# A fused attention and two-MLP kernel: each attention lane packs all its units before it unpacks them

## The chip, the core and the metric

The kernel runs on one core of one Trainium2 chip. The metric is the device time of one execution in microseconds (us). The engines are PE (TensorE matmul), PEld (its weight load), DVE (VectorE), ACT (ScalarE), POOL (GpSimd) and SP (SyncE, which issues every DMA here). Each works through its own program in order, and semaphores hold an instruction until what it reads is there.

## The reference

Shapes: q, k, v are 4 x 8 x 576 x 64 and p is 4 x 8 x 32 x 64 (batch, head, token, depth).

```python
def sm_attn(qq, kk, vv):
    s = scale * qq @ kk.T;  s = s - max(s);  a = exp(s)
    return (a / (sum(a) + 1e-9)) @ vv
p_packed = sm_attn(p, k, v)                  # "pack":   32 rows attend to 576
x = sm_attn(q, p_packed, p_packed)           # "unpack": 576 rows attend to 32
x = x.transpose(0, 2, 1, 3).reshape(2304, 512)
h = x @ w_in;  x = (h * sigmoid(1.702 * h)) @ w_out       # first MLP, 512 -> 2048 -> 512
pr = domain_probs / (domain_probs.sum(-1) + 1e-9)         # second MLP: four experts
out = sum(pr[:, e] * (relu(x @ w1[e]) @ w2[e]) for e in range(4))
```

w_in and w_out come as 64-bit floats, which the kernel turns into pairs of 32-bit numbers ("conversions").

## The kernel before

The attention is cut into eight units: a unit is one batch and four of its heads. Unit u has two steps. `pack(u)` (written p0 to p7) turns k with PE (tile kT), takes scores against pT (ps_s), the maximum on DVE (st), the exponential on ACT, turns the result back (ps_e), multiplies it with v (ps_v), divides on DVE (pp) and turns that once more (ps_pt). `unpack(u)` (u0 to u7) does the like for q (qT, then t on DVE), takes the exponential on ACT, multiplies on POOL and leaves the tile a, cast on ACT (L446) and finished on DVE (L448).

A conversion works on one 512 KB piece of w_in or w_out: six DVE operations (all write the tile cvt), one on POOL, a cast on ACT and a subtraction on POOL. Eight pieces serve the first quarter of the hidden width, four more follow in the same lane (`MORE`).

The first MLP runs in four rounds, one for a quarter of the hidden width, and eight half-batches j in a round. `packed_w` (ps_w) multiplies the packed rows of four units with w_in, ACT and DVE copy it out (pw, L482 and L486); `l1_first` (ps_h) multiplies that with the tiles a of the two units of a batch, ACT applies the gelu twice (L516, L517), DVE subtracts (h, L520); `l2_first` (ps_acc) multiplies with w_out, and ACT copies into y. A half-batch is four groups of 6 ps_h and 12 ps_acc matmuls.

The order in which these stand in the engines' programs is made when the program is written. The class `Order` keeps several parts side by side: two attention lanes (`LANES`), a lane of conversions and the lane of the first MLP. Each part says which engine it wants next and for how long by its own table; `Order.run` takes the one that can start first, and a lower rank on ties. The instructions are then written in that order for all engines ("the head"); after it a scheduler or a fixed loop takes over. All loads are issued by SP in one order (`FIRST`, then as lanes ask for them). Tiles of the pool `big` (29 slots) are handed out in the same order, and a load waits in SP's queue until its slot is free.

In the kernel before, a lane packs two units and unpacks them, then does the same with its other two. The probabilities are loaded by `norm_probs`, which is written after the head, but its load stands second in SP's program.

Of the kernel before, what the change touches and what calls it, by code (L numbers as in the profile page):

```python
# [19 lines left out]

LANES = ("p0 p2 u0 u2 p4 p6 u4 u6", "p1 p3 u1 u3 p5 p7 u5 u7")
FIRST = "k0 k1 F F F F k2 k3 q0 q1 F F F F"
HOP = 0.25
UNITS_DONE = 6
MORE = 4


class Order:

    def __init__(self, banks):
        self.free = banks
        self.at = {}
        self.parts = []
        self.on = False

    def add(self, part, rank, at=0.0):

        if not self.on:  # L40
            return self.drain(part)
        self.parts.append([rank, at, next(part, None), part])

# [8 lines left out]
    def run(self, while_):  # L52
        self.on = True
        while while_():
            best = None
            for p in self.parts:
                rank, at, ask, part = p
                if callable(ask):
                    t = ask()
                    if t is None:  # L60
                        continue
                    p[1] = max(at, t)
                    p[2] = self.send(p, p[1])
                    best = p
                    start = None
                    break
# [6 lines left out]
            if start is None:  # L73
                continue
            assert best is not None, [p[2] for p in self.parts]
            (start, _), p = best
            engine, us, banks = p[2]
            self.free -= banks
            self.at[engine] = start + us
            p[1] = start + us + HOP  # L80
            p[2] = self.send(p, p[1])
        self.on = False
# [15 lines left out]
def packed_attention_moe_kernel(  # L98
# [13 lines left out]
    nc = tc.nc  # L112
# [33 lines left out]
    def slot(shape, dt, name):  # L146
        return big.tile(shape, dt, tag="b", name=name)
# [49 lines left out]
    def convert():  # L197
# [12 lines left out]
        f32 = man.bitcast(F32)  # L210
        yield "DVE", 0.83, 0

# [6 lines left out]
        )  # L219
        yield "DVE", 1.2, 0  # L220
        nc.vector.tensor_scalar(
# [25 lines left out]
    def load_kv(u):  # L247

        b, g = units[u]
        h0 = G * g  # L250
        sl = [slot([SP, 3 * R * D], F32, f"kv{u}{i}") for i in range(3)]
        m = 2 * R * D
        raws["k", u] = []
# [11 lines left out]
        raws["v", u] = [sl[0][:, m:], sl[1][:, m:], sl[2][:, :R * D], sl[2][:, R * D:m]]  # L265

# [12 lines left out]
    def transposed_scores(pair, dst, scores):  # L279

        for s in range(2):
            for j in range(2):
                yield "PE", 0.4, 1
                ps = psum("ps_t")
                for r in range(3):
                    nc.tensor.transpose(ps[:, r * SP:(r + 1) * SP], pair[j][3 * s + r], ident[:SP, :SP])
                t = yield "ACT", 0.4, 0
                nc.scalar.copy(out=dst[:, j, s * HS:(s + 1) * HS], in_=ps[:, :HS])
                order.free += 1
        for s in range(2):  # L290
            yield "PE", 0.6, 1
            yield from scores(s)
# [39 lines left out]
    def pack(u):  # L332
        b, g = units[u]
        kr, vr = raws.pop(("k", u)), raws.pop(("v", u))
        st = small.tile([128, 8], F32, tag="st", bufs=4, name=f"st{u}")
        kT = slot([128, 2, S], F32, f"kT{u}")
# [13 lines left out]
        for s in range(2):  # L350
            yield "ACT", 0.7, 0
            nc.scalar.activation(
# [10 lines left out]
        for s in range(2):  # L363
            yield "PE", 0.45, 1
            ps = psum("ps_e")
# [6 lines left out]
            order.free += 1  # L372
        yield "PE", 1.0, 1
        ps = psum("ps_v")
# [40 lines left out]
    def unpack(u):  # L415
# [17 lines left out]
        nc.vector.tensor_sub(out=t, in0=t, in1=s2[:, 0, :].unsqueeze(2).to_broadcast([128, NB, NP]))  # L433
        yield "ACT", 0.7, 0
        nc.scalar.activation(out=t, in_=t, func=AF.Exp, scale=scale)
# [23 lines left out]
    def packed_w(a, bp):  # L459

        for g in range(UG):
# [11 lines left out]
            for b in (2 * bp, 2 * bp + 1):  # L473
                PW[a, b, g] = slot([128, 2, 512], F32R, f"pw{g}")
            order.add(packed_w_out(a, bp, g, pss), 1, clock())

# [16 lines left out]
    def l1_first(a, j, c):  # L493
# [16 lines left out]
        h = hid[a, j, c // 2][:, 2 * (c % 2):2 * (c % 2) + 2, :]  # L510
        order.add(l1_out(h, ps), 1, clock())

    def l1_out(h, ps):
# [5 lines left out]
        yield "DVE", 0.47, 0  # L519
        nc.vector.tensor_sub(out=h[:, 1, :], in0=g32, in1=h[:, 0, :].bitcast(F32))  # L520

    def l2_first(a, j, t):
# [21 lines left out]
        order.add(l2_out(a, j, t, ps), 1, clock())  # L544

# [245 lines left out]
    def reads(fn, args):  # L791
# [6 lines left out]
        return [("out", args[0], c) for c in range(CPP)]  # L798

# [68 lines left out]
    with tc.manual_schedule(engines=engines):  # L868
# [15 lines left out]
    norm_probs()  # L884
    t_parts = {i: t_sums(i) for i in range(NPAIR)}
# [71 lines left out]
```

## Time and profile before

| | us |
|---|---|
| median of 3 runs (lowest to highest) | 1238.83 (1236.79 to 1240.83) |
| profiled execution: its time | 1239.21 |
| profiled execution: span of the trace | 1237.4 |
| PE busy (matmul), of the span | 1174.5 (95%) |
| DVE busy | 913.6 (74%) |
| ACT busy | 522.9 (42%) |
| POOL busy | 486.5 (39%) |

An engine's busy time is the union of its instructions. Matmuls are pipelined, so a busy PE can still be slow: the granted clock (1.00 is 2.4 GHz, 0.50 is 1.2 GHz, a number between is a mean over both) has to be read beside it. Windows are given in us from the start of the span.

### The profile page before, as it was taken

Reading aid. Unit: us, or ns where it says so; the run is one execution under the profiler, and the core shown is the slowest. Engines: PE = TensorE matmul, PEld = TensorE weight load, DVE = VectorE, ACT = ScalarE, POOL = GpSimd, SP = SyncE. Lnnn points to the kernel's source line nnn. Section 1 sums busy time; section 2 is a strip of 40 time slices with the busy share of each in tenths; the row PEclk is TensorE's granted clock in tenths of the full one; section 3 lists DMA queues with packets and bytes.
Section 4 is the critical chain, followed back from the end, with each engine's and each line's share of the span. In section 5 each row is a group of like instructions: output and inputs, shape, how many; then the busy total and the mean of one; then the engine's idle time right before and its main releaser. Section 6 shows DMA issues by size and latency. Waiting matters only on the chain.

```text
span 1237.4 us, 18457 instructions
## 1 busy us (share of the span) xinstructions
PE 1174.5 (95%) x6912; PEld 1059.5 (86%) x6912; DVE 913.6 (74%) x1646; ACT 522.9 (42%) x1152; POOL 486.5 (39%) x415
## 2 busy tenths in 40 slices
PE   6769878999999989999999999999999999999998
PEld 4457667999999989999999989999999789999997
DVE  4873478787786675777777977777778867777775
ACT  3557654444434444333333344333333443333331
POOL 1320023221121244444444765444447644444441
PEclk9879789999999999999999999999999999999999
DMA  8623212120210002222222132222221232222211
GB/s 233 181 77 78 73 52 85 52 69 18 80 40 18 1 17 69 68 68 69 69 69 68 51 110 95 69 68 68 69 69 35 67 121 69 69 69 69 68 52 51
DMA packets 90393, 87.47 MB, mean 71 GB/s; under 512 B 43968, under 2 KB 71616, under 8 KB 90304
## 3 DMA queue, kind: packets, MB, share of 16 engines
q1 hardware_dynamic: 90304, 86.30, 23.3%
q8 instruction: 54, 0.88, 0.3%
q14 instruction: 35, 0.29, 0.1%
HBM read 81.56 MB, written 4.72 MB: 70 GB/s over the span
## 4 chain that ended last, share of the span: by engine, by line
PE 76%; DVE 4%; ACT 2%; issue 1%; POOL 0%; DVEq 0%
PE ps_o L726 30%; PE ps_p L674 27%; PE ps_acc L528 12%; PE ps_h L500 6%; DVE b L609 1%; PE ps_w L468 1%; ACT h L682 1%; DVE o L737 1%; ACT b L608 0%; DVE s L643 0%; DVE h L520 0%; ACT w L153 0%; DVE h L683 0%; POOL w L154 0%; DVE u L700 0%
## 5 line engine op out<-in xcount | busy, mean ns | idle before, releaser
L726 PE MATMUL ps_o<-w,h 128*128 128x512 f32 x1728 | 444.5, 393 | 0.0
L674 PE MATMUL ps_p<-b,w 128*128 128x384 f32 x2016 | 402.9, 338 | 4.9 <-POOL w L154 2.6
L674 PEld LDWEIGHTS ps_p<-b,w 128*128 128x128 f32 x2016 | 360.1, 188 | 32.1 <-POOL w L154 4.6
L726 PEld LDWEIGHTS ps_o<-w,h 128*128 128x128 f32 x1728 | 321.9, 188 | 50.2
L154 POOL TENSOR_TENSOR w<-raw,w 128x512 fp32r<-128x512 f32 x192 | 230.1, 1198 | 227.8 <-ACT w L153 222.9
L737 DVE SCALAR_TENSOR_TENSOR o<-ps_o,pr,o 128x512 f32<-128x512 f32 x270 | 201.5, 746 | 48.0 <-PE ps_o L726 48.0
L528 PE MATMUL ps_acc<-h,wout 128*128 128x288 f32 x1536 | 231.6, 298 | 5.0 <-DVE h L520 5.0
L528 PEld LDWEIGHTS ps_acc<-h,wout 128*128 128x128 f32 x1536 | 213.7, 190 | 9.3 <-DVE h L520 6.4
L154 POOL TENSOR_TENSOR w<-s,w 128x512 fp32r<-128x512 f32 x96 | 125.2, 1304 | 164.3 <-ACT w L153 164.3
L500 PE MATMUL ps_h<-a,pw 128*128 128x288 f32 x768 | 129.0, 303 | 17.4 <-ACT a L446 12.6
L500 PEld LDWEIGHTS ps_h<-a,pw 128*128 128x128 f32 x768 | 112.5, 193 | 21.2 <-ACT a L446 13.4
L520 DVE TENSOR_TENSOR h<-g,h 128x288 fp32r<-128x288 f32 x128 | 73.0, 572 | 61.9 <-ACT g L517 61.5
L153 ACT CAST w<-s 128x512 fp32r<-128x512 f32 x96 | 58.9, 614 | 126.0 <-DVE s L646 126.0
L153 ACT CAST w<-raw 128x512 fp32r<-128x512 f32 x192 | 106.6, 555 | 1.7 <-DMA raw<-in_moe_w_dram 1.6
L516 ACT ACTIVATE h<-ps_h 128x288 fp32r<-128x288 f32 x128 | 53.1, 415 | 105.2 <-PE ps_h L500 104.7
L217 POOL TENSOR_SCALAR cvt<-cvt 128x512 uint32<-128x512 uint32 x32 | 23.9, 747 | 128.7 <-DVE cvt L214 110.2
L682 ACT ACTIVATE h<-c 128x384 fp32r<-128x384 f32 x48 | 25.3, 527 | 106.9 <-DVE c L708 106.9
L682 ACT ACTIVATE h<-u 128x384 fp32r<-128x384 f32 x48 | 25.2, 525 | 71.6 <-DVE u L714 71.6
L553 DVE TENSOR_TENSOR y<-ps_acc,y 128x288 f32<-128x288 f32 (+2 forms) x120 | 44.8, 389 | 12.9 <-PE ps_acc L528 12.7
L682 ACT ACTIVATE h<-uv 128x384 fp32r<-128x384 f32 x48 | 25.3, 526 | 67.2 <-DVE uv L714 67.2
L643 DVE TENSOR_TENSOR s<-raw 128x256 f32<-128x256 f32 x48 | 45.1, 941 | 10.4 <-DMA raw<-in_moe_w_dram 10.4
L517 ACT ACTIVATE g<-ps_h 128x288 f32<-128x288 f32 x128 | 52.6, 411 | 0.1
(100 smaller groups left out, 1162.9 us busy)
## 6 DMA issues: line engine op xcount, KB each, us to landing
raw<-in_moe_w_dram SPq DMA_DIRECT2D x96, 512.0 KB, 4.0
raw<-in_moe_w_in_dram SPq DMA_DIRECT2D x16, 512.0 KB, 3.9
raw<-in_moe_w_out_dram SPq DMA_DIRECT2D x16, 512.0 KB, 3.7
kv<-in_k_dram SPq DMA_DIRECT2D x32, 144.0 KB, 3.2
q<-in_q_dram SPq DMA_DIRECT2D x32, 144.0 KB, 2.8
out_dram<-o SPq DMA_DIRECT2D x18, 256.0 KB, 2.0
kv<-in_v_dram SPq DMA_DIRECT2D x16, 144.0 KB, 3.0
kv<-in_v_dram SPq DMA_DIRECT2D x8, 288.0 KB, 3.4
```

Of the source, the lines that this page charges most:

```text
L153: nc.scalar.copy(out=hi, in_=src)
L154: eng.tensor_sub(out=lo, in0=src, in1=hi.bitcast(F32))
L500: nc.tensor.matmul(out=ps[:, :HS], lhsT=PW[a, b, g][:, wp, c * 128:(c + 1) * 128], rhs=A[b * UG + g][:, xp, s * HS:(s + 1) * HS], start=(m ...
L516: nc.scalar.activation(out=h[:, 0, :], in_=ps[:, :HS], func=AF.Gelu_apprx_sigmoid)
L517: nc.scalar.activation(out=g32, in_=ps[:, :HS], func=AF.Gelu_apprx_sigmoid)
L520: nc.vector.tensor_sub(out=h[:, 1, :], in0=g32, in1=h[:, 0, :].bitcast(F32))
L528: nc.tensor.matmul(out=ps[:, :HS], lhsT=W["out", a, c][:, wp, t * 128:(t + 1) * 128], rhs=hid[a, j, c // 2][:, 2 * (c % 2) + hq, :], start ...
L643: nc.vector.tensor_add(out=s1, in0=Am["A21"], in1=Am["A22"])
L674: nc.tensor.matmul(out=ps, lhsT=Wop[n, a, wp, kk], rhs=Bop[i, b, xp, kk], start=(m == 0), stop=(m == 5),)
L682: nc.scalar.activation(out=h[:, 0, :], in_=src, func=AF.Relu)
L726: nc.tensor.matmul(out=ps, lhsT=h[:, c, hq, o:o + 128], rhs=W2[n, c][:, wp, :], start=(c == 0 and m == 0), stop=(c == 1 and m == 2),)
L737: nc.vector.scalar_tensor_tensor(out=acc, in0=ps, scalar=pr[:, tok, e:e + 1], in1=acc, op0=ALU.mult, op1=ALU.add,)
```

## The change

Each lane now packs its four units and then unpacks them. `Order` looks for the earliest start plus a handicap per part instead of breaking ties by rank, adds 1.28 us of its own reckoning where an ACT step would need another function table than the last one ("exp" or "gelu"), and a part whose condition is met is no longer served at once. Some of the planner's table times are changed. The k and v of units 0, 1 and 2 are loaded into the three buffers of the pool `yp`, which later hold y, so nine of the 29 slots of `big` stay free at the start. The pool `small` has 4 buffers instead of 2. The load of the probabilities moves behind the loads of `FIRST`, and `norm_probs` runs after the head. No arithmetic is changed. The program has 8 table loads on ACT where it had 18.

```diff
-LANES = ("p0 p2 u0 u2 p4 p6 u4 u6", "p1 p3 u1 u3 p5 p7 u5 u7")
+LANES = ("p0 p2 p4 p6 u0 u2 u4 u6", "p1 p3 p5 p7 u1 u3 u5 u7")
+EARLY = (0, 1, 2)
+TABLE = 1.28
...
-                engine, us, banks = ask
+                engine, us, banks, table = (p[2] + (None,))[:4]
                 if banks > self.free:
                     continue
-                start = max(at, self.at.get(engine, 0.0))
-                if best is None or (start, rank) < best[0]:
-                    best, start_ = ((start, rank), p), start
+                start = max(p[1], self.at.get(engine, 0.0))
+                late = TABLE if table not in (None, self.table) else 0.0
+                if best is None or start + late + p[0] < best[0]:
+                    best = start + late + p[0], start + late + us, p
...
-    small = ctx.enter_context(tc.tile_pool(name="small", bufs=2))
+    small = ctx.enter_context(tc.tile_pool(name="small", bufs=4))
...
-        yield "DVE", 1.2, 0
+        yield "DVE", 1.5, 0
...
+        if u in EARLY:
+            t = yp.tile([128, KD, 2 * TB], F32, tag="y", name=f"kv{u}").rearrange("p k t -> p (k t)")
+            sl = [t[:SP, x * 3 * n:(x + 1) * 3 * n] for x in range(2)] + [t[:SP, 6 * n:8 * n]]
+        else:
+            sl = [slot([SP, 3 * n], F32, f"kv{u}{i}") for i in range(3)]
...
-            yield "ACT", 0.7, 0
+            yield "ACT", 0.7, 0, "exp"
...
-        yield "ACT", 0.82, 0
+        yield "ACT", 0.82, 0, "gelu"
...
     def norm_probs():
-        nc.sync.dma_start(out=pr, in_=probs.rearrange("(t p) e -> p t e", p=128))
...
         load(FIRST)
+        nc.sync.dma_start(out=pr, in_=probs.rearrange("(t p) e -> p t e", p=128))
         order.on = True
         lanes = [lane(x) for x in LANES] + [conversions(2 * CPP, MORE)]
-        for i, x in enumerate(lanes):
-            order.add(x, 2 + i)
-        order.add(moe_lane(), 9)
+        for x in lanes[:-1]:
+            order.add(x, 0.0)
+        order.add(lanes[-1], 0.6)
+        order.add(moe_lane(), 0.3)
```

Three places show what the new order does (the digit behind kT, q, kv, pp, t or a is the unit, what follows the underscore is a serial number).

PE behind the last matmul of unit 3's pack (ps_pt of pp3), before the change:

```order
L400 MATMUL ps_pt_565<-ident_76,pp3_557 128x128
L286 MATMUL ps_t_573<-ident_76,q0_160 128x96 x3
L297 MATMUL ps_s_588<-qT0_508,pT_78 64x288 x2
L286 MATMUL ps_t_592<-ident_76,q1_163 128x96 x3
L468 MATMUL ps_w_597<-win_181,ppw0_302 128x512 x3
L468 MATMUL ps_w_601<-win_252,ppw0_302 128x512 x3
L297 MATMUL ps_s_611<-qT0_508,pT_78 64x288 x2
```

The same place after it:

```order
L407 MATMUL ps_pt_567<-ident_76,pp3_560 128x128
L293 MATMUL ps_t_576<-ident_76,kv40_395 128x96 x3
L293 MATMUL ps_t_585<-ident_76,kv41_396 128x96 x3
L293 MATMUL ps_t_592<-ident_76,kv50_428 128x96 x3
L475 MATMUL ps_w_610<-win_176,ppw0_308 128x512 x3
L475 MATMUL ps_w_614<-win_253,ppw0_308 128x512 x3
L304 MATMUL ps_s_620<-kT4_524,pT_78 64x288 x2
```

The unpacks of units 0 and 1 stood here; now the packs of units 4 and 5 do, and those of units 6 and 7 behind them. Counting matmuls further on, the last score of an unpack stands behind 114 ps_h, 168 ps_acc and 24 ps_w matmuls before, and behind 84, 120 and 12 after; from the second round of the MLP on, PE's order is the same in both.

ACT at the exponentials (L352) of the pack of unit 4, before:

```order
L352 ACT_TABLE_LOAD
L352 ACTIVATE kT4_882,st4_881<-ps_s_976,st4_881 128x288
L352 ACTIVATE kT4_882,st4_881<-ps_s_992,st4_881 128x288
L288 COPY kT5_1009<-ps_t_1011 128x288
L516 ACT_TABLE_LOAD
```

And after:

```order
L489 CAST pw1_642<-ps_w_637 64x512
L359 ACTIVATE kT4_524,st4_523<-ps_s_620,st4_523 128x288
L295 COPY kT5_583<-ps_t_665 128x288
L359 ACTIVATE kT4_524,st4_523<-ps_s_646,st4_523 128x288
L378 COPY kv40_395<-ps_e_694 96x384
```

No gelu stands before or between them any more, so the two table loads are gone. The unpacks keep three of these pairs of loads.

DVE behind the last division of unit 5's pack (pp5), before the change:

```order
L387 SCALAR_TENSOR_TENSOR pp5_1286<-ps_v_1256,st5_1008,mask2_77 128x128
L343 TENSOR_REDUCE st6_1143<-ps_s_1283 128x1
L347 TENSOR_SCALAR st6_1143<-st6_1143 128x1
L358 TENSOR_SCALAR st6_1143<-st6_1143 128x1
L361 RECIPROCAL st6_1143<-st6_1143 128x1
L520 TENSOR_TENSOR h_1248<-g32_1331,h_1248 128x288
```

And after:

```order
L394 SCALAR_TENSOR_TENSOR pp5_800<-ps_v_767,st5_582,mask2_77 128x128
L214 TENSOR_SCALAR cvt_795<-raw_169 128x512
L215 TENSOR_SCALAR cvt_795<-cvt_795 128x512
L222 TENSOR_SCALAR cvt_795<-raw_169 128x512
L225 SCALAR_TENSOR_TENSOR cvt_795<-raw_169,cvt_795 128x512
L229 SCALAR_TENSOR_TENSOR cvt_795<-raw_169,cvt_795 128x512
L232 SCALAR_TENSOR_TENSOR cvt_795<-cvt_795 128x512
L350 TENSOR_REDUCE st6_764<-ps_s_844 128x1
L350 TENSOR_REDUCE st6_764<-ps_s_855 128x1
L354 TENSOR_SCALAR st6_764<-st6_764 128x1
L350 TENSOR_REDUCE st7_818<-ps_s_866 128x1
```

Before, packs 6 and 7 stood among the MLP's subtractions (L520). Now one conversion, the eighth, is left here, and behind it DVE has only the steps of packs 6 and 7 and then those of unpacks 0 and 1.

## Rows read from the trace of the kernel before

**Rows 1.** The page, part 2: busy tenths in 40 slices of 30.9 us

```profile
PE   6769878999999989999999999999999999999998
```

**Rows 2.** Windows: from:to, length; PE, PEld, DVE, ACT, POOL busy; clock; DMA; GB/s

```profile
18.00:47.20 29.20, 21.03 (x269) 13.88 (x266) 24.64 (x55) 15.03 (x47) 13.23 (x17) 0.90 0.92 254
47.20:76.60 29.40, 16.22 (x77) 10.26 (x78) 27.14 (x44) 14.15 (x31) 9.15 (x10) 0.67 0.37 95
76.60:153.80 77.20, 69.84 (x619) 56.15 (x619) 34.98 (x76) 58.06 (x141) 5.88 (x11) 0.87 0.30 76
153.80:216.00 62.20, 47.86 (x333) 44.46 (x329) 49.67 (x86) 32.09 (x77) 18.59 (x17) 0.94 0.22 66
```

**Rows 3.** Waits of PE from 18 to 216 us: total, times, longest

```profile
PE ps_h L500 <- ACT a L446: 12.6, 3, 8.6
```

**Rows 4.** Timeline of PE, 186 to 260 us: start, length, operation, idle before

```profile
203.67 2.93 PE L468 MATMUL ps_w<-win,ppw 128*128 128x512 f32 x12
...
215.96 0.61 PE L500 MATMUL ps_h<-a,pw 128*128 128x288 f32 x1 [4.57 <-ACT pw L482]
...
223.90 0.96 PE L500 MATMUL ps_h<-a,pw 128*128 128x288 f32 x6
...
226.28 0.95 PE L500 MATMUL ps_h<-a,pw 128*128 128x288 f32 x6
```

**Rows 5.** Timeline of SP's queue from 0 us: DMA issues

```profile
1.25 0.56 SPq L751 DMA_DIRECT2D pr<-in_moe_domain_probs_dram  x1
1.85 3.87 SPq L257 DMA_DIRECT2D kv<-in_k_dram  x4
...
7.37 2.71 SPq L257 DMA_DIRECT2D kv<-in_k_dram  x4
```

**Rows 6.** Timeline of DVE: unit 3's division, unit 1's last subtraction

```profile
47.17 0.35 DVE L387 SCALAR_TENSOR_TENSOR pp<-ps_v,st,mask 128x128 f32<-128x128 f32 x1 [1.24 <-PE ps_v L377]
...
75.85 1.14 DVE L448 TENSOR_TENSOR a<-t,a 128x576 fp32r<-128x576 f32 x1 [0.43 <-ACT a L446]
```

**Rows 7.** Windows, the tile st alone (four packs): DVE, ACT

```profile
76.60:153.80 77.20, 7.23 (x24) 4.55 (x16) 0.87 0.30 76
```

**Rows 8.** Lines of DVE, 18 to 76.6 us: busy, mean ns

```profile
L486 DVE TENSOR_TENSOR pw<-ps_w,pw 64x512 fp32r<-64x512 f32 x8 | 5.5, 688 | 0.2
```

**Rows 9.** Timeline of ACT, units 7 (kT, pT) and 4 (qT)

```profile
128.52 0.40 ACT L288 COPY kT<-ps_t 128x288 f32<-128x288 f32 x1 [1.33 <-PE ps_t L286]
...
132.07 1.28 ACT L352 ACT_TABLE_LOAD   x1
133.37 0.50 ACT L352 ACTIVATE kT<-ps_s,st 128x288 f32<-128x288 f32 x1
...
134.62 0.70 ACT L288 COPY qT<-ps_t 128x288 f32<-128x288 f32 x2
...
140.98 0.27 ACT L402 COPY pT<-ps_pt 128x128 f32<-128x128 f32 x1
```

**Rows 10.** Timeline of DVE: the last subtraction of unit 4's unpack

```profile
145.59 0.76 DVE L448 TENSOR_TENSOR a<-t,a 128x576 fp32r<-128x576 f32 x1
```

**Rows 11.** Timeline of PE: a score at either clock, three transposes

```profile
12.68 1.23 PE L297 MATMUL ps_s<-kT,pT 128*64 128x288 f32 x4
...
83.97 0.41 PE L286 MATMUL ps_t<-ident,q 96*128 96x96 f32 x3
...
85.14 0.71 PE L297 MATMUL ps_s<-qT,pT 128*64 128x288 f32 x4
```

**Rows 12.** Windows, all engines, 10 us about the MLP's first matmuls

```profile
70.00:80.00 10.00, 7.20 (x32) 5.62 (x31) 8.69 (x15) 5.62 (x11) 3.04 (x3) 0.55 0.40 106
```

**Rows 13.** Windows, the tile cvt alone (seven conversions): DVE, ACT, POOL

```profile
153.80:216.00 62.20, 26.64 (x42) 4.35 (x7) 14.85 (x14) 0.94 0.22 66
```

**Rows 14.** Windows, the tile t alone (three unpacks): DVE, ACT, POOL

```profile
153.80:216.00 62.20, 13.72 (x21) 4.08 (x6) 3.73 (x3) 0.94 0.22 66
```

**Rows 15.** Windows, the tile h alone: PE, PEld, DVE, ACT

```profile
153.80:216.00 62.20, 29.67 (x192) 27.18 (x192) 9.12 (x16) 6.85 (x16) 0.94 0.22 66
```

More of the change, by code (lines that the diff above doesn't have):

```diff
@@ L36, in __init__, with add @@
         self.on = False
-    def add(self, part, rank, at=0.0):
+        self.table = None
+    def add(self, part, handicap, at=0.0):
         if not self.on:
             return self.drain(part)
-        self.parts.append([rank, at, next(part, None), part])
+        self.parts.append([handicap, at, next(part, None), part])
     def drain(self, part):
@@ L55, in run @@
             best = None
[L56 to L59, printed above, removed]
+            for p in list(self.parts):
+                while callable(p[2]):
+                    t = p[2]()
                     if t is None:
-                        continue
-                    p[1] = max(at, t)
+                        break
+                    p[1] = max(p[1], t)
                     p[2] = self.send(p, p[1])
-                    best = p
-                    start = None
-                    break
-                engine, us, banks = ask
+                if p not in self.parts or callable(p[2]):
+                    continue
+                engine, us, banks, table = (p[2] + (None,))[:4]
                 if banks > self.free:
                     continue
-                start = max(at, self.at.get(engine, 0.0))
-                if best is None or (start, rank) < best[0]:
-                    best, start_ = ((start, rank), p), start
-            if start is None:
-                continue
+                start = max(p[1], self.at.get(engine, 0.0))
+                late = TABLE if table not in (None, self.table) else 0.0
+                if best is None or start + late + p[0] < best[0]:
+                    best = start + late + p[0], start + late + us, p
             assert best is not None, [p[2] for p in self.parts]
-            (start, _), p = best
-            engine, us, banks = p[2]
+            _, end, p = best
+            engine, us, banks, table = (p[2] + (None,))[:4]
             self.free -= banks
-            self.at[engine] = start + us
-            p[1] = start + us + HOP
+            self.at[engine] = end
+            self.table = table or self.table
+            p[1] = end + HOP
             p[2] = self.send(p, p[1])
@@ L210, in convert @@
         f32 = man.bitcast(F32)
-        yield "DVE", 0.83, 0
+        yield "DVE", 0.9, 0
         nc.vector.tensor_scalar(out=ex, in0=hi, scalar1=0x7FF00000, scalar2=None, op0=ALU.bitwise_and)
@@ L250, in load_kv @@
         h0 = G * g
-        sl = [slot([SP, 3 * R * D], F32, f"kv{u}{i}") for i in range(3)]
         m = 2 * R * D
+        n = R * D
+        if u in EARLY:
[3 more added lines that the diff above has]
+            sl = [slot([SP, 3 * n], F32, f"kv{u}{i}") for i in range(3)]
         raws["k", u] = []
@@ L264, in load_kv @@
         arrives(("k", u), 1.18)
-        raws["v", u] = [sl[0][:, m:], sl[1][:, m:], sl[2][:, :R * D], sl[2][:, R * D:m]]
+        raws["v", u] = [sl[0][:, m:], sl[1][:, m:], sl[2][:, :n], sl[2][:, n:m]]
     def load_q(u):
@@ L282, in transposed_scores @@
             for j in range(2):
-                yield "PE", 0.4, 1
+                yield "PE", 0.5, 1
                 ps = psum("ps_t")
@@ L290, in transposed_scores @@
         for s in range(2):
-            yield "PE", 0.6, 1
+            yield "PE", 0.9, 1
             yield from scores(s)
@@ L334, in pack @@
         kr, vr = raws.pop(("k", u)), raws.pop(("v", u))
-        st = small.tile([128, 8], F32, tag="st", bufs=4, name=f"st{u}")
+        st = small.tile([128, 8], F32, tag="st", name=f"st{u}")
         kT = slot([128, 2, S], F32, f"kT{u}")
@@ L363, in pack @@
         for s in range(2):
-            yield "PE", 0.45, 1
+            yield "PE", 0.7, 1
             ps = psum("ps_e")
@@ L372, in pack @@
             order.free += 1
-        yield "PE", 1.0, 1
+        yield "PE", 1.5, 1
         ps = psum("ps_v")
@@ L433, in unpack @@
         nc.vector.tensor_sub(out=t, in0=t, in1=s2[:, 0, :].unsqueeze(2).to_broadcast([128, NB, NP]))
-        yield "ACT", 0.7, 0
+        yield "ACT", 0.7, 0, "exp"
         nc.scalar.activation(out=t, in_=t, func=AF.Exp, scale=scale)
@@ L474, in packed_w @@
                 PW[a, b, g] = slot([128, 2, 512], F32R, f"pw{g}")
-            order.add(packed_w_out(a, bp, g, pss), 1, clock())
+            order.add(packed_w_out(a, bp, g, pss), 0.0, clock())
     def packed_w_out(a, bp, g, pss):
@@ L510, in l1_first, with l1_out @@
         h = hid[a, j, c // 2][:, 2 * (c % 2):2 * (c % 2) + 2, :]
-        order.add(l1_out(h, ps), 1, clock())
-    def l1_out(h, ps):
-        yield "ACT", 0.82, 0
+        order.add(l1_out(("h", a, j, c), h, ps), 0.0, clock())
+    def l1_out(key, h, ps):
+        yield "ACT", 0.82, 0, "gelu"
         g32 = gp.tile([128, HS], F32, tag="g", name="g32")
@@ L518, in l1_out @@
         order.free += 1
-        yield "DVE", 0.47, 0
+        t_ = yield "DVE", 0.47, 0
         nc.vector.tensor_sub(out=h[:, 1, :], in0=g32, in1=h[:, 0, :].bitcast(F32))
+        when[key] = t_
     def l2_first(a, j, t):
@@ L543, in l2_first @@
                     ACC[i] = yp.tile([128, KD, 2 * TB], F32, tag="y", name=f"y{i}")
-        order.add(l2_out(a, j, t, ps), 1, clock())
+        order.add(l2_out(a, j, t, ps), 0.0, clock())
     def l2_out(a, j, t, ps):
@@ L797, in reads @@
             return [("a", b * UG + g) for g in range(UG)] + [("pw", args[0], b, g) for g in range(UG)]
-        return [("out", args[0], c) for c in range(CPP)]
+        return [(x, args[0]) + y + (c,) for c in range(CPP) for x, y in (("out", ()), ("h", (args[1],)))]
     def moe_step():
@@ L883, in packed_attention_moe_kernel @@
             order.finish(p)
-    norm_probs()
+        norm_probs()
     t_parts = {i: t_sums(i) for i in range(NPAIR)}
```

## The prediction

> **What bounds the kernel now.** I read the page's slices first [rows 1]. From the eighth slice on PE is busy nearly throughout, and PE's order there is not touched; in the first seven (216 us) it is not. So the change can win or lose only there, and one event closes that stretch: the first ps_h matmul of the MLP's second round, at 215.96 us [rows 4]. PE must do the same matmuls ahead of it in both kernels, and what follows runs at PE's own pace. Whatever that event moves by, the end moves by.
>
> The windows cut the stretch by what DVE and PE do [rows 2]. From 18 to 76.6 us DVE is the busy engine: 24.64 of 29.2 and 27.14 of 29.4 us, with PE at 21.0 and 16.2 us, in the second window at a granted clock of 0.67. From 76.6 to 153.8 us it is the other way round: DVE is busy 34.98 of 77.2 us, and PE 69.84, at a clock of 0.87. From 153.8 us on DVE is busy again for 49.67 of 62.2 us. So 42 us of idle DVE lie in the middle, where the second four packs crawl along between matmuls of the MLP, and then DVE's work piles up at the end: the last unpacks and seven conversions, for which PE waits. The waits confirm it. PE's largest, 12.6 us in three, is ps_h for the tile a of an unpack [rows 3], and the event itself comes after 4.57 us of idle, waiting for pw [rows 4], which stands behind the conversions on DVE. The lever is thus the order of work, not a duration.
>
> **The change, part by part.** I follow the event through six terms. "pp3" is unit 3's division, at 47.2 us now; "a1" is the end of unit 1's unpack, at 77.0 us [rows 6], from which on the MLP's matmuls run.
>
> (1) Start to pp3. The probabilities' load leaves the front of SP's queue: its own issue takes 0.56 us, and the four k issues behind it take 3.87 us where the next four take 2.71 [rows 5]. If PE's first transposes gain all of that, 1.7 us are won; if the loads are bounded by bandwidth, none. I take 1.2: pp3 at 46.0. That the first three units' k and v lie in the buffers of y, and that `small` has more buffers, costs no instruction. It frees nine slots, so that the loads of units 4 and 5 wait for nothing late. The last load of unit 7 waits for unit 4's last ps_v, by terms (2) and (3) some 15 us ahead of its own use, which leaves room for a transfer.
>
> (2) pp3 to pp5. The packs of units 4 and 5 stand here now. DVE has in this stretch two conversions at 26.64 / 7 = 3.8 us [rows 13], eight subtractions of pw at 0.69 [rows 8], and two packs at 7.23 / 4 = 1.8 [rows 7]: 7.6 + 5.5 + 3.6 = 16.7 us. At the fill of the window from 18 us on (24.64 / 29.2 = 0.84, [rows 2]) that is 19.9: pp5 at 65.9. Bounds: 16.7 with DVE full, 24 at a fill of 0.7.
>
> (3) pp5 to pp7. One conversion is left as cover: 3.8 + 3.6 = 7.4 us of DVE work, so here the chain through ACT and PE decides. Unit 7 alone took from its last kT copy at 128.52 to its pT at 140.98, 12.5 us, with a table load of 1.28 us in it [rows 9]. Two units side by side share that chain; I add half of the eight kT copies (8 x 0.4 / 2 = 1.6) and the stagger, and take off the load: 13 us, pp7 at 78.9. Bounds: 9 and 17.
>
> The load is where I weighed a rule of the Trainium skill. In the row it ends at 133.35 and the exponential starts at 133.37: a switch costs 1.28 us and nothing else [rows 9]. "ScalarE: Activation LUTs", section "What ACT_TABLE_LOAD costs", gives about 2.66 us, a drain included. By that page, as an estimate, this term would be 11.6 us and the forecast 1.4 us lower. No drain shows in the rows, so the row decides.
>
> (4) pp7 to a1. Unpacks 0 and 1 run without cover. Unit 4's took from its last qT copy (135.32) to its last subtraction (146.35), 11.0 us [rows 9, 10]. Ahead of it stand eight copies (3.3 us), and the second unit ends later by about half its DVE work of 13.72 / 3 = 4.6 us [rows 14]: 16.6 (bounds 14.3 and 18.5). So a1 at 95.5, against 77.0: the MLP starts 18.5 us later. That is the price of the change. Bounds for a1: 86 with the lower ends, 107 with the upper ones.
>
> (5) a1 to the last scores of unpacks 6 and 7. PE has 84 ps_h and 120 ps_acc matmuls, 19 groups of three transposes and 12 scores. Six ps_h and twelve ps_acc take 2.38 us [rows 4], so 204 / 18 x 2.38 = 27.0; 19 x 0.41 = 7.8 and 12 x 0.71 = 8.5 [rows 11]: 43.3 us at the full clock. The four packs no longer stand between them, ACT has 10 x 1.28 us of table loads fewer, and units 2 to 5 finish while PE has the matmuls of the pair before. But PE comes out of a thin stage. Around the MLP's start the clock was 0.55 [rows 12]; ten such microseconds give up about 4.5. I take 48: 143.5. Bounds: 43 and 55 (two waits for a of 3 to 4 us left).
>
> (6) Last scores to the event. DVE has 38 operations of conversions (24.1 us by [rows 13]), two unpacks (9.1, [rows 14]), 18 subtractions of h at 9.12 / 16 = 0.57 (10.3, [rows 15]), eight of pw (5.5, [rows 8]) and about 1 us that I allow for small rows: 50 us, as much as the 49.67 of the window that does this now. PE has 324 / 18 x 2.38 = 42.8 and two rounds of ps_w at 2.9 [rows 4]: 48.6. So neither has slack. With DVE full it takes 50, at today's fill (49.67 / 62.2) 62.5. Today's window has the longest wait of PE for an unpack in it, 8.6 us [rows 3], which then holds up DVE too; without the most of it, 57. The event comes at 200.5.
>
> Sum: 200.5 - 216.0 = -15.5 us. Against the profiled execution's own 1239.2 us that is 1223.7; this execution lies 0.4 above the median, which changes nothing. I say 1224.
>
> **The rivals.**
> More gained: DVE is as full in (2) as its work allows, the chains in (3) and (4) overlap, and a1 comes at 88. Then the event is at 193 or earlier and the time 1210 to 1217. For it: DVE's 42 idle us are large enough. Against: pairs of chains have nothing beside them in (3) and (4).
>
> The tail gives back: (6) runs at today's fill, because the conversions wait for slots of `big` and DVE's own order, and the event comes at 206 to 212: 1229 to 1235. For it: the 4.57 us wait at the event is of just that kind [rows 4]. With (5) at its upper end as well nothing remains: 1235 to 1243. By this case the removed table loads lay on an engine that had time anyway, ACT being busy 58 of 77 us [rows 2].
>
> Slower, by the clock. PE idles more until a1, and stage (5) mixes short transposes and scores with matmuls. If the granted clock in (5) stayed at the 0.67 of the window from 47 to 77 us [rows 2], its 43.3 us would become 65 and the event 217; from a mean clock below 0.64 in (5) the kernel is slower (43.3 / 0.64 = 67.7, event at 220), and at 0.55 the time is 1254. The Trainium skill, "TensorE: Matmul & The Clock Gate", Part 1, calls the throttled clock the default that only sustained activity releases, which speaks for it. By it the first matmuls of (5) run at 1.2 GHz, and the row at 0.55 agrees [rows 12]; how long this lasts is open. Against: the same mix of matmuls and packs from 76.6 to 153.8 us had 0.87 [rows 2].
>
> **How the numbers follow.** My forecast (1217 to 1229) has 0.45, more gained 0.14, the tail giving back (1229 to 1235) 0.18, nothing left 0.12, slower 0.11. A measurement of this kernel tells about 0.3% (3.7 us) from no change. Faster by more than that: 0.45 + 0.14 + 0.18 = 0.77; within: 0.12; slower: 0.11. The range reaches from the middle of "more gained" to the upper edge of "nothing left": 1213 to 1240. The bounds of the terms, added up, would reach from 1202 to 1248; that all of them err to one side is what I leave out.
>
> **What would show it.** In the profile of the changed kernel: pp3 at about 46, pp7 at about 79 and a1 at 93 to 98 us; DVE idle for some 30 us in (3) to (5), against the 42 of the middle window now; only three pairs of table loads behind a1; the last scores at 140 to 148; the event at 197 to 205, still behind a wait for pw. From there to the end 1021 us as now. A wait of PE for a load of k or q over 3 us, a1 beyond 105, or a clock under 0.7 in (5) would make the forecast wrong; a shift after the event would make the whole frame wrong.

## The result, and the profile after

The changed kernel takes 1224.32 us (median of 4 runs, 1223.37 to 1225.05), the kernel before 1238.19 us beside it: a ratio of 0.9885, 95% interval 0.9866 to 0.9904, so it is 14 us faster. The forecast was 1224 us. The profiled execution took 1225.05 us, with a span of 1223.2 us, and the rows below are of it.

The page's slices, PE, DVE and the granted clock (a slice is 30.6 us now):

```profile
PE   5787998999999999999999999999999999999998
DVE  4756886887875856777777877777778867777775
PEclk8778998999999999999999999999999999999999
```

Against [rows 1] the first four slices of PE are together no fuller (27 tenths for 28). The fifth and sixth are (9 and 9 for 8 and 7), and from there on the rows differ by one tenth in one slice. The event of the prediction, the first ps_h of the MLP's second round, stands at 200.27 us instead of 215.96 [rows 4]:

```profile
139.22 0.66 PE L293 MATMUL ps_t<-ident,q 96*128 96x96 f32 x6
139.66 1.05 PE L536 MATMUL ps_acc<-h,wout 128*128 128x288 f32 x6
140.55 0.41 PE L293 MATMUL ps_t<-ident,q 96*128 96x96 f32 x3
140.90 2.16 PE L304 MATMUL ps_s<-qT,pT 128*64 128x288 f32 x16
142.99 3.06 PE L475 MATMUL ps_w<-win,ppw 128*128 128x512 f32 x12
...
200.27 0.61 PE L507 MATMUL ps_h<-a,pw 128*128 128x288 f32 x1 [5.01 <-ACT pw L489]
```

From the event to the end of the span are 1022.9 us, against 1021.4 before: the whole gain is made ahead of the event. The 1.5 us more behind it are within what the kernels below differ by there (1019 to 1023 us).

DVE's timeline has the steps of the sum, the divisions of units 3, 5 and 7 and unit 1's last subtraction (start, length, operation, idle before):

```profile
46.87 0.34 DVE L394 SCALAR_TENSOR_TENSOR pp<-ps_v,st,mask 128x128 f32<-128x128 f32 x1
...
71.10 0.35 DVE L394 SCALAR_TENSOR_TENSOR pp<-ps_v,st,mask 128x128 f32<-128x128 f32 x1 [1.38 <-PE ps_v L384]
...
85.23 0.35 DVE L394 SCALAR_TENSOR_TENSOR pp<-ps_v,st,mask 128x128 f32<-128x128 f32 x1 [2.01 <-PE ps_v L384]
...
100.45 0.76 DVE L455 TENSOR_TENSOR a<-t,a 128x576 fp32r<-128x576 f32 x1 [0.78 <-ACT a L453]
```

So pp3 came at 46.9 (forecast 46.0), pp5 at 71.1 (65.9), pp7 at 85.2 (78.9), a1 at 101.2 (95.5), the last scores at 143.0 (143.5) and the event at 200.3 (200.5). The sum came out, but term (2) is 4.3 us too short and term (5) 6.2 us too long: that they cancel is luck.

PE's waits from 18 to 216 us (total, times, longest), which answer to [rows 3]:

```profile
PE ps_e L375 <- ACT kT L359: 9.9, 4, 3.9
PE ps_h L507 <- ACT a L453: 8.0, 2, 4.7
PE ps_h L507 <- ACT pw L489: 5.0, 1, 5.0
PE ps_t L293 <- DMA kv<-in_k_dram: 4.5, 3, 2.3
```

In the kernel before, the wait for the exponentials was

```profile
PE ps_e L368 <- ACT kT L352: 4.3, 4, 2.5
```

The waits for a fell from 12.6 to 8.0 us, and a wait of 8.4 us ahead of unit 1's scores is gone (its row stands further down, with the planner's parts). The wait for the exponentials of packs that now run side by side grew from 4.3 to 9.9 us, and a new one came, for k of units 4 and 5 (4.5 us in three, the longest 2.3).

**An account that holds for every kernel here.** Up to the event each kernel does the same work: 1332 or 1333 matmul records and 136 to 141 us of DVE. The event is therefore PE's busy time plus PE's idle time. The windows up to the event (from:to, length, then PE, PEld, DVE, ACT, POOL busy, clock, DMA, GB/s), first of the kernel before, then of the changed one:

```profile
0.00:100.00 100.00, 68.78 (x530) 48.86 (x531) 69.68 (x138) 53.56 (x126) 25.39 (x34) 0.86 0.61 161
100.00:215.96 115.96, 96.19 (x804) 82.53 (x804) 69.89 (x132) 71.31 (x180) 22.11 (x26) 0.90 0.25 68
0.00:215.96 215.96, 164.97 (x1332) 131.39 (x1333) 139.56 (x270) 124.87 (x305) 47.50 (x60) 0.88 0.42 111
```

```profile
0.00:100.00 100.00, 66.67 (x676) 43.21 (x676) 60.18 (x128) 47.57 (x137) 26.83 (x40) 0.76 0.68 176
100.00:200.27 100.27, 92.35 (x656) 84.62 (x656) 77.78 (x142) 65.88 (x159) 21.53 (x20) 0.96 0.23 64
0.00:200.27 200.27, 159.02 (x1332) 127.82 (x1332) 137.97 (x270) 113.44 (x295) 48.36 (x60) 0.86 0.45 120
```

PE idled 215.96 - 164.97 = 51.0 us before and 41.25 after: 9.7 of the 15.7 us are idle time, 6.0 are the same matmuls done in less time. These are one execution each; three kernels below with the same lanes and nearly the same time (no_table, no_early, pr_front) have 160.6 to 162.3 us of busy time, so of the 6.0 us some 3 can be chance.

### The profile page after: what moved, and what is told of

Read it like the earlier page. It is cut to its first block, busy times and chain, and to the rows that moved or that the text cites. A ratio compares the mean times of both kernels' runs of the same rounds, so it can differ in the third digit from the quotient of the medians.

```text
span 1223.2 us, 18425 instructions
## 1 busy us (share of the span) xinstructions
PE 1168.7 (96%) x6912; PEld 1053.7 (86%) x6912; DVE 911.7 (75%) x1646; ACT 511.4 (42%) x1142; POOL 487.5 (40%) x415
## 4 chain that ended last, share of the span: by engine, by line
PE 81%; DVE 6%; ACT 3%; issue 2%; POOL 1%; DMA 1%; DVEq 0%; POOLq 0%; ACTq 0%
PE ps_o L734 29%; PE ps_p L682 25%; PE ps_acc L536 16%; PE ps_h L507 8%; PE ps_w L475 2%; DVE b L617 1%; ACT h L690 1%; PE ps_s L304 1%; DVE o L745 1%; POOL w L155 1%; DMA raw<-in_moe_w_dram 1%; DVE h L691 1%; PE ps_t L293 1%; ACT b L616 0%; ACT w L154 0%
## 5 line engine op out<-in xcount | busy, mean ns | idle before, releaser
L690 ACT ACTIVATE h<-u 128x384 fp32r<-128x384 f32 x48 | 25.2, 525 | 71.5 <-DVE u L722 71.5
```

The costliest lines, as they stand in the source:

```text
L690: nc.scalar.activation(out=h[:, 0, :], in_=src, func=AF.Relu)
```

## The experiments

The prediction's reason was that packing first fills DVE's idle time in the middle. The rivals tried against it: the new planner makes the gain whatever the lanes, fewer table loads make it, or the freed buffers and the load's place do. Times are medians, each ratio is to the kernel before on the same chip; event, busy and idle time are of the one profiled execution, which lay up to 3.2 us off its kernel's median (ol_plan, 1230.93 against 1227.75).

| kernel | us | ratio, 95% interval | event | PE busy + idle |
|---|---|---|---|---|
| before | 1238.19 | 1 | 215.96 | 165.0 + 51.0 |
| before_costs | 1234.73 | 0.9982 (0.9973 to 0.9991) | 211.48 | 165.3 + 46.2 |
| before_hand | 1234.19 | 0.9973 (0.9960 to 0.9987) | 210.25 | 165.9 + 44.4 |
| before_both | 1233.71 | 0.9970 (0.9961 to 0.9980) | 209.81 | 166.5 + 43.3 |
| ol_outs | 1234.38 | 0.9975 (0.9965 to 0.9986) | 210.68 | 160.7 + 50.0 |
| ol_plan | 1227.75 | 0.9921 (0.9906 to 0.9937) | 208.18 | 161.4 + 46.7 |
| ol_table0 | 1228.99 | 0.9933 (0.9920 to 0.9946) | 205.20 | 162.6 + 42.6 |
| oldlanes | 1227.16 | 0.9911 (0.9892 to 0.9929) | 203.80 | 162.5 + 41.3 |
| no_table | 1225.48 | 0.9893 (0.9877 to 0.9910) | 203.45 | 162.3 + 41.2 |
| no_early | 1224.27 | 0.9886 (0.9867 to 0.9904) | 201.02 | 160.6 + 40.4 |
| pr_front | 1224.92 | 0.9884 (0.9866 to 0.9903) | 202.89 | 162.1 + 40.8 |
| changed | 1224.32 | 0.9885 (0.9866 to 0.9904) | 200.27 | 159.0 + 41.3 |
| more0_k45 | 1230.30 | 0.9935 (0.9921 to 0.9949) | 207.02 | 164.8 + 42.3 |
| k45_first | 1220.58 | 0.9858 (0.9843 to 0.9873) | 197.18 | 159.8 + 37.4 |

In all fourteen the span ends 1019 to 1023 us after the event. That part of the prediction's frame held: what the event gains, the kernel gains.

### oldlanes: the lanes alone undone

```diff
-LANES = ("p0 p2 p4 p6 u0 u2 u4 u6", "p1 p3 p5 p7 u1 u3 u5 u7")
+LANES = ("p0 p2 u0 u2 p4 p6 u4 u6", "p1 p3 u1 u3 p5 p7 u5 u7")
```

> The changed kernel with the old order of the lanes (two packs, two unpacks, two packs, two unpacks each); the new planner, the buffers and the place of the probabilities' load stay. Theory (the gain is idle DVE time in the middle that is filled because all packs come first): the hole comes back, DVE is idle about 40 us between the first a and unit 7's pack, the first ps_h of round 2 comes at 211 to 216 us, 1233 to 1240 us in all. Rival (the planner and the buffers make the gain, the lanes little): event at 200 to 204, 1224 to 1228 us.

Measured: 1227.16 us, 0.9911, event at 203.80. My theory fell here. With the old lanes the MLP starts at 69 us (before 72.5), and yet 11 of the 14 us of gain are there. The hole in DVE came back only in part: from a1 to unit 7's pack DVE idles 28.2 of 59.4 us, where it idled 38.4 of 64.3 in the kernel before. The windows of oldlanes:

```profile
0.00:100.00 100.00, 73.29 (x581) 50.41 (x582) 69.86 (x139) 52.05 (x134) 26.45 (x36) 0.86 0.63 164
100.00:203.80 103.80, 89.21 (x753) 80.14 (x751) 67.68 (x131) 66.85 (x167) 21.17 (x24) 0.94 0.26 73
0.00:203.80 203.80, 162.50 (x1332) 130.55 (x1332) 137.54 (x270) 118.91 (x299) 47.62 (x60) 0.90 0.44 118
```

Against the changed kernel PE idles 26.7 instead of 33.3 us up to 100 us, and 14.6 instead of 7.9 us from there to the event: packing first moves 6.6 us of idle time from behind to the front and removes none. PE's busy time is 3.5 us less in the changed kernel. The windows by tile show where: the 528 matmuls of ps_h and ps_acc up to the event took 91.9 us in oldlanes and 84.8 in the changed kernel. In oldlanes 80 of them stand in the first 100 us and take 17.7 us, 0.22 us each; the others take 0.165. In the changed kernel all but one stand behind, at 0.16 each and a granted clock of 0.96. That the lanes save this busy time isn't shown: in the table, changed, no_early, pr_front and no_table, with the new lanes, lie at 159.0 to 162.3 us, and oldlanes and its variants (names with ol_), with the old ones, at 160.7 to 162.6. What the eight share is the new planner; the four kernels with the old one or parts of the new lie at 165.0 to 166.5 (more0_k45, with the new planner and the new lanes, at 164.8). By the medians the lanes are worth 0.26%, and the two intervals overlap.

### no_table and ol_table0: the planner's price of a table load at 0, with the new and with the old lanes

```diff
-TABLE = 1.28
+TABLE = 0.0
```

> The changed kernel with the planner's price of a table load at 0 instead of 1.28; everything else stays. Theory: the loads lie on ACT, which has time; they come back (12 to 18 instead of 7), the event moves by 0 to 4 us, 1224 to 1229 us. Rival (the gain comes from fewer table loads, ten of 1.28 us): event 8 to 13 us later, 1232 to 1238 us.

> The changed kernel with the old lanes and the price of a table load at 0. Theory: as with the price, event at 202 to 208, 1225 to 1230 us, with 14 to 18 table loads instead of 12. Rival (under the old lanes the price of loads is what makes the gain): event at 211 to 216, 1234 to 1240 us.

Measured: 1225.48 us, event at 203.45, with 11 loads behind the first one instead of 7; and 1228.99 us, event at 205.20, with 17 instead of 11. The price is worth about 1 us with the new lanes and 2 with the old, neither clear of its interval. The loads lie on an engine that has time, as the prediction said.

### no_early, pr_front and ol_plan: the buffers and the load's place

```diff
-EARLY = (0, 1, 2)
+EARLY = ()
```

> The changed kernel with k and v of units 0 to 2 in the shared slots again instead of the buffers of y. Theory of the prediction (nine free slots let the loads of units 4 and 5 go on): without them these loads wait for slots, pp5 comes 5 to 10 us later than 71.1, the event 4 to 10 us later, 1228 to 1235 us. Rival (those loads are late because of all that is queued in front of them, slots or not): pp5 within 2 us of 71.1, 1224 to 1226 us.

```diff
+        nc.sync.dma_start(out=pr, in_=probs.rearrange("(t p) e -> p t e", p=128))
         all_p()
         load(FIRST)
-        nc.sync.dma_start(out=pr, in_=probs.rearrange("(t p) e -> p t e", p=128))
```

> The changed kernel with the probabilities' load ahead of everything again, as in the kernel before. By term (1) of the prediction pp3 comes about 1 us later than 46.9 and the event as much: 1225 to 1226 us. Rival (in its new place, just ahead of unit 4's k, the load with its many small packets holds those up): the four k of unit 4 are issued in 3 to 5 us instead of 8.4, pp5 comes 2 to 4 us earlier than 71.1 and the event 1 to 3 us earlier: 1221 to 1223 us.

Measured: 1224.27 and 1224.92 us, neither to be told from the changed kernel. In no_early pp5 comes at 70.7 us (end) against 71.5: the loads of units 4 and 5 do not wait for slots, with or without the nine freed ones. In pr_front the four k of unit 4 are issued in 5.5 instead of 8.4 us, but the v behind them in 5.0 instead of 1.4, and the row ends at 47.7 against 46.5 us: the queue is behind as a whole, and which row shows it is chance. pp3 ends at 47.9 against 47.2. A difference of that size can't be told at the end: the medians differ by 0.6 us. ol_plan undoes all of this with the old lanes, and so leaves only the planner with its costs and weights:

> The changed kernel with the old lanes, and also with k and v of units 0 to 2 in the shared slots, two buffers for the small tiles and the probabilities' load in front, all as in the kernel before: what is left of the change is the planner with its costs and weights. Theory now (under the old lanes the planner makes the gain): event at 202 to 206, 1226 to 1229 us. Rival (the buffers and the load's place make the part that the costs and weights alone did not): event at 207 to 212, 1231 to 1236 us.

Measured: 1227.75 us, 0.9921. The event of its profiled execution (208.18) fell into the rival's range, but that execution was the slowest of its six; the median decides for the theory. The planner alone, without new lanes, buffers or load, makes 10 of the 14 us. The reverse, the new lanes with the old planner, was not run, so what they would be worth by themselves stays open.

### before_costs, before_hand, before_both and ol_outs: which part of the planner

Under the old planner a part's rank decided ties, and a tie is the common case: all parts that wait for an engine can start when it comes free. In the trace of before a conversion's work stood ahead of a unit's, on DVE and then on ACT:

```profile
65.98 0.62 ACT L235 CAST wout<-cvt 128x512 fp32r<-128x512 f32 x1 [5.99 <-DVE cvt L231]
66.99 0.67 ACT L446 CAST a<-t 128x576 fp32r<-128x576 f32 x1 [0.39 <-DVE t L443]
68.59 0.68 ACT L435 ACTIVATE t<-t 128x576 f32<-128x576 f32 x1 [0.93 <-DVE t L433]
69.18 0.98 ACT L288 COPY qT<-ps_t 128x288 f32<-128x288 f32 x3
```

```profile
69.61 2.48 PE L297 MATMUL ps_s<-qT,pT 128*64 128x288 f32 x8 [8.38 <-DVE cvt L213]
```

The copies of qT stand behind a cast of wout that waits 5.99 us for DVE and two steps of a unit, and PE's scores of that unpack, which read qT, start at 69.61 us after 8.38 us of idle. (The row names a step of DVE as what released PE, but the scores don't read its tile; the first copy of qT, begun at 69.18 us, ends at about the same time. That reading is argued from the times.) The first two kernels give the old planner one new part each, the third both.

```diff
-        yield "DVE", 0.83, 0
+        yield "DVE", 0.9, 0
...
-        yield "DVE", 1.2, 0
+        yield "DVE", 1.5, 0
```

> The kernel before with the six new costs alone (conversion 0.9 and 1.5 for 0.83 and 1.2, pack steps 0.5, 0.9, 0.7, 1.5 for 0.4, 0.6, 0.45, 1.0); planner, lanes and buffers of before. Theory: dearer conversions put fewer of them ahead of a unit's step, part of the gain: event at 208 to 214, 1230 to 1237 us. Rival (rule, table price or buffers do it): event within 2 us of 216, 1236 to 1240 us.

```diff
-                if best is None or (start, rank) < best[0]:
-                    best, start_ = ((start, rank), p), start
+                late = start + {4: 0.6, 9: 0.3}.get(rank, 0.0)
+                if best is None or (late, rank) < best[0]:
+                    best, start_ = ((late, rank), p), start
...
+            start -= {4: 0.6, 9: 0.3}.get(p[0], 0.0)
```

> The kernel before, its lanes, buffers, costs and old planner, with one thing of the new planner: 0.6 us are added to the start of the conversions and 0.3 us to that of the MLP's lane when the planner compares candidates. Theory now (with the old lanes the gain comes from how the planner places the conversions against the units' steps on DVE): PE's wait of 8.4 us for unit 1's scores goes, a1 comes at 72 to 74 instead of 77, the event at 204 to 209 instead of 216, 1226 to 1232 us. Rival (the price of table loads or the buffers do it): event within 2 us of 216, 1236 to 1240 us.

> The kernel before with the added 0.6 and 0.3 us and the six new costs, without table price, buffers, place of the probabilities' load or new lanes. Theory: nearly all of the gain of the new planner under the old lanes (event 203.8, 1227.2): event at 202 to 208, 1225 to 1231 us. Rival (table price or buffers needed): 1234 to 1240 us.

Measured: 1234.73, 1234.19 and 1233.71 us. Each gives some 0.2 to 0.3%, and both together hardly more than one: they do not add up, and the rest of the planner's 0.8% is elsewhere. The theory's ranges for before_hand and before_both were missed by 2 to 3 us. The kernel ol_outs tries the ties: the steps that empty the MLP's PSUM banks had rank 1 and won every tie; in the new list they are added last and lose them.

```diff
-        order.add(l1_out(("h", a, j, c), h, ps), 0.0, clock())
+        order.add(l1_out(("h", a, j, c), h, ps), -0.01, clock())
```

(The same for packed_w_out and l2_out, with the old lanes.)

> The changed kernel with the old lanes, and with a handicap of -0.01 instead of 0 for the steps that take the MLP's results out of PSUM, so that they win ties, as their rank 1 did in the old planner; under the new one they lose ties to the units. Theory (this change of ties is a part of the gain, about 4 us): event at 206 to 210, 1229 to 1234 us. Rival (ties do nothing): event at 202 to 206, 1225 to 1229 us.

Measured: 1234.38 us, 0.9975: 7 to 8 of oldlanes' 11 us are gone. The rows show how. ACT of ol_outs, from 173 us on:

```profile
173.64 0.41 ACT L523 ACTIVATE h<-ps_h 128x288 fp32r<-128x288 f32 x1 [0.40 <-PE ps_h L507]
173.94 0.41 ACT L524 ACTIVATE g<-ps_h 128x288 f32<-128x288 f32 x1
175.25 0.40 ACT L559 COPY y<-ps_acc 128x288 f32<-128x288 f32 x1 [0.90 <-PE ps_acc L536]
175.65 1.28 ACT L442 ACT_TABLE_LOAD   x1
176.95 0.68 ACT L442 ACTIVATE t<-t 128x576 f32<-128x576 f32 x1
```

There are two such exponentials. DVE had the second's input ready by 163.1 us, 12.6 us ahead of the table load, and the first's before that:

```profile
162.32 0.76 DVE L440 TENSOR_TENSOR t<-t,s 128x576 f32<-128x576 f32 x1
```

and PE paid for it behind:

```profile
181.96 0.61 PE L507 MATMUL ps_h<-a,pw 128*128 128x288 f32 x1 [6.74 <-ACT a L453]
```

Ahead of the exponential stand the gelus and copies of the MLP, one after the other, each winning its tie; the price of the table load helps them, since a gelu finds its table loaded and the exponential doesn't. PE waits 16.7 us in five for a, in oldlanes 8.1 in two. The old planner's ties with the price at 0 were not tried apart. Nor were two more of the planner's changes: a part whose condition is met no longer goes at once, and a step of the MLP's second layer now also waits for the planner's time of the h that it reads. So ties are shown to be able to cost this much, and not that they make all the rest of the gain.

### k45_first and more0_k45: the loads of k on the path, and the stretch ahead of the event

```diff
-FIRST = "k0 k1 F F F F k2 k3 q0 q1 F F F F"
+FIRST = "k0 k1 F F F F k2 k3 k4 k5 F F F F"
...
                 (load_kv if t[0] == "k" else load_q)(int(t[1]))
+                if t == "q1":
+                    nc.sync.dma_start(out=pr, in_=probs.rearrange("(t p) e -> p t e", p=128))
...
         load(FIRST)
-        nc.sync.dma_start(out=pr, in_=probs.rearrange("(t p) e -> p t e", p=128))
```

> The changed kernel with k and v of units 4 and 5 loaded right behind those of units 2 and 3, the second four F behind them, q of units 0 and 1 and the probabilities after the last k. Theory (the 4.3 us that term (2) missed are the late loads of k of units 4 and 5, and they lie on the path): PE's waits for k under 1.5 us instead of 4.5, pp5 at 65 to 68 instead of 71.1, pp7 at 79 to 82 instead of 85.2, event at 195 to 198, 1218 to 1222 us. Rival (another wait takes their place, for the second four F or on DVE): pp5 within 1.5 us of 71, event at 199 to 202, 1223 to 1226 us.

Measured: 1220.58 us, 0.9858, event at 197.18, the fastest kernel here. SP's queue of the changed kernel, where the k of unit 4 and then of unit 5 follow the probabilities:

```profile
28.59 4.88 SPq L281 DMA_DIRECT2D q<-in_q_dram  x8
33.51 2.24 SPq L191 DMA_DIRECT2D raw<-in_moe_w_out_dram  x4
35.79 0.66 SPq L883 DMA_DIRECT2D pr<-in_moe_domain_probs_dram  x1
36.49 8.42 SPq L264 DMA_DIRECT2D kv<-in_k_dram  x4
...
46.62 2.88 SPq L264 DMA_DIRECT2D kv<-in_k_dram  x4
```

and of k45_first, where they stand ahead of the second four F (the last row is the k of unit 6):

```profile
26.57 3.27 SPq L264 DMA_DIRECT2D kv<-in_k_dram  x4
...
31.48 2.83 SPq L264 DMA_DIRECT2D kv<-in_k_dram  x4
...
35.96 2.05 SPq L191 DMA_DIRECT2D raw<-in_moe_w_out_dram  x4
38.13 5.72 SPq L264 DMA_DIRECT2D kv<-in_k_dram  x4
```

The k of unit 4 are all issued at 29.8 instead of 44.9 us. PE's wait of 4.5 us for them is gone (0.9 us of another wait for k is left), and pp5 comes at 66.8 us:

```profile
66.82 0.35 DVE L394 SCALAR_TENSOR_TENSOR pp<-ps_v,st,mask 128x128 f32<-128x128 f32 x1 [1.38 <-PE ps_v L384]
```

The event moved by 3.1 us and the median by 3.7, and pp5 by 4.3, so these loads lay on the path. The intervals of the two ratios just overlap (0.9873 and 0.9866); the four runs of either kernel don't (1218.5 to 1221.3 against 1223.4 to 1225.1 us).

The other kernel adds to this:

```diff
-MORE = 4
+MORE = 0
```

> The kernel with k of units 4 and 5 loaded early, and without the four conversions ahead (MORE = 0), which are then made when they are due. Theory of term (6) (DVE is full from the last scores to the event): 4 x 3.8 = 15 us of DVE work leave that stretch, it shrinks from 58 to 49 to 52 us, PE's own 48.6 us then being the bound, and the event comes 6 to 9 us earlier than in the kernel without this; from the event to the end no more than 1026 us: 1212 to 1217 us. Rival 1 (DVE is not what bounds the stretch): event within 2 us of the kernel without this. Rival 2 (the conversions then stand ahead of work that PE waits for later): the event is earlier, but from it to the end it takes 1028 us or more.

Measured: 1230.30 us, event at 207.02, 10 us later than in k45_first. The premise was wrong: the four conversions are pieces of w_in for the second quarter of the hidden width, and the event itself reads the pw made from them. Nothing left the stretch; the work was only moved to its end. But the rows tell what the wait ahead of the event is. ACT of more0_k45:

```profile
200.67 0.62 ACT L236 CAST wout<-cvt 128x512 fp32r<-128x512 f32 x1 [3.92 <-DVE cvt L232]
205.27 0.62 ACT L236 CAST wout<-cvt 128x512 fp32r<-128x512 f32 x1 [3.98 <-DVE cvt L232]
205.79 0.57 ACT L489 CAST pw<-ps_w 64x512 fp32r<-64x512 f32 x1
```

and of the changed kernel:

```profile
195.30 0.40 ACT L559 COPY y<-ps_acc 128x288 f32<-128x288 f32 x1 [0.90 <-PE ps_acc L536]
198.52 0.62 ACT L236 CAST wout<-cvt 128x512 fp32r<-128x512 f32 x1 [2.82 <-DVE cvt L232]
199.04 1.18 ACT L489 CAST pw<-ps_w 64x512 fp32r<-64x512 f32 x2
```

The casts of pw, which PE waits for, stand on ACT behind casts of wout, whose conversions DVE has not finished. Three such casts stand ahead of them in more0_k45 (the first, at 196.12 us, without a wait) and PE waits 11.5 us; one in the changed kernel, and it waits 5.0. The wout is needed only later. A kernel with pw's casts ahead was not run.

## Why the prediction came out, and where its steps failed

The time was right, and the frame (one event, and what it gains the end gains) held in every kernel. The reason given was wrong in its main part, and the sum came out because two terms erred by 4 and 6 us in opposite directions. Of the signs that were named, pp7 (79, measured 85.2), a1 (93 to 98, measured 101.2) and DVE's idle time in (3) to (5) (some 30 us, measured 23.5) failed; the last scores, the event with its wait for pw, the clock in (5) and the waits for k came as said. The range ends at 1240 us, not at the upper edge of "nothing left", which is 1243.

**"The lever is thus the order of work": right, but not the order that the prediction meant.** It laid the gain to the packs coming first, into the 42 us of idle DVE. The planner with the old lanes makes 10 to 11 of the 14 us. The new lanes add about 3 to that, and not clear of the intervals. Idle time of DVE was no measure of what could be won: PE's idle time in front grew by as much as that behind shrank. The prediction costed the planner's new rule at nothing but table loads; that ties, costs and handicaps change which step goes first on every engine is what it left out. Nor did it price the second-longest wait of PE before, 8.4 us in one ahead of unit 1's scores, which is gone in the changed kernel (in oldlanes one of 5.9 us for scores is left).

**Term (1), 1.2 us: took 0.3, and the size stays open.** pp3 came 0.3 us earlier than before, and putting the load back changed no time that could be told. But single executions differ by more: with the new planner pp3 starts at 46.1 to 46.9 us in seven of the eight kernels that load the probabilities later (48.5 in no_table), and at 47.6 and 48.0 in the two that load them first (pr_front, ol_plan).

**Term (2), 19.9 us: took 24.2,** just beyond its upper bound of 24. The work on DVE was costed well: with k of units 4 and 5 early, pp3 to pp5 takes 20.5 us (46.3 to 66.8). "The loads of units 4 and 5 wait for nothing late" failed: not for slots, but for what is queued ahead of them. That is q of units 0 and 1, which nobody needs until 85 us, and the second four F; k45_first moved both, so their shares are not told apart.

**Terms (3) and (4), 13 and 16.6 us: took 14.1 and 16.0.** a1 is 24.2 us later than before, and the price of the change was foreseen as 18.5; of the difference of 5.7 us, 4.3 are term (2)'s.

**Term (5), 48 us: took 41.8.** That is less than the 43.3 us which the prediction worked out for the full clock, though the granted clock was 0.94 and PE had no idle time:

```profile
101.20:143.00 41.80, 41.80 (x308) 36.04 (x307) 30.40 (x58) 30.61 (x73) 5.43 (x5) 0.94 0.21 55
```

So the single prices were too high. The PE rows at 139 us show why: six transposes are a row of 0.66 us, but the next row starts 0.44 us behind their start; three are a row of 0.41 and the next starts after 0.35; sixteen matmuls of scores are a row of 2.16 and the next starts after 2.09, so four take 0.52, not 0.71. A row's duration counts the time in which the next has begun.

**Term (6), 57 us: took 57.3.** The size was right, its reason only in part. "So neither has slack" is half true. For 30 us ahead of the last wait PE runs through at the full clock, while DVE has time left, in the window from 166 to 196 us:

```profile
166.00:196.00 30.00, 29.26 (x211) 28.52 (x209) 23.49 (x47) 15.47 (x43) 9.83 (x10) 1.00 0.23 71
```

PE is what bounds there. The wait at the event is one of order on ACT. The prediction had seen that pw stands behind conversions, on DVE; the rows place it one engine further.

**The rivals.** The tail gave nothing back, the clock in (5) held, and fewer table loads were worth 1 to 2 us. The true rival, that the planner alone does it, was not among them.

## What to carry to other kernels

When a change moves an order and also the rule that makes orders, price them apart: build the new rule with the old order before explaining the gain by the order. To judge an order, add up the busy and the idle time of the engine that bounds, up to the event that closes the stretch, by stage; idle time on another engine says little of what is to be won. Look at who wins ties in a planner, and at each in-order queue for the step behind which the awaited one stands: a load not needed for 50 us, or a cast that waits for a slow producer.

## What the runs showed of the hardware

A small load can take long. The probabilities' 36 KB took 7.9 us from issue to landing in the changed kernel, k's loads of 144 KB a median of 3.8. Moving it changed no time that could be told. The queue behind it was late in either place: the DMA engines' share from 18 to 47.2 us was 0.90 here and 0.92 before [rows 2].

A table load's cost beside its 1.28 us is again not to be seen: in ol_outs the load ends at 176.93 and the exponential starts at 176.95, as in [rows 9]. The Trainium skill, "ScalarE: Activation LUTs", section "What ACT_TABLE_LOAD costs", gives about 2.66 us with a drain; these rows don't show it.

The granted clock rose while PE's busy share fell. The windows of the changed kernel behind pp3:

```profile
65.00:78.00 13.00, 10.42 (x90) 6.92 (x90) 9.74 (x21) 6.78 (x21) 5.92 (x8) 0.50 0.25 69
78.00:95.00 17.00, 12.29 (x174) 7.96 (x173) 8.52 (x21) 8.37 (x28) 2.35 (x5) 0.97 0.62 140
```

From 65 to 78 us PE is busy 10.4 of 13 us at 0.50, the lower level (1.2 GHz); from 78 to 95 us it is busy 12.3 of 17 us, at nearly the full one. The shares can't be compared as amounts of work, since the same matmuls take longer at the lower level (four scores 1.23 us against 0.71 [rows 11]): by count PE ran 90 matmuls in the 13 us and 174 in the 17. No run varied this by itself, so what raised the clock stays open.

The same DVE operation on the same shape, L215 on 128x512, took 0.41 us at its shortest and 1.52 at its longest in the first 200 us of the changed kernel (15 of them). What stretches it was not tried.
